# Attention, soft mixture of experts and squared-ReLU layer on one core: nine multiplications by the softmax reciprocals move from VectorE to GpSimd

## The chip, the cores and the metric

The kernel runs on one core of a Trainium2 chip. The metric is the device time of one execution in microseconds (us). TensorE (PE in the profile; PEld is its weight load), VectorE (DVE), ScalarE (ACT), GpSimd (POOL) and SyncE (SP) each work through a queue of their own in program order and wait for each other on semaphores. GpSimd's queue here also issues DMAs.

## The reference

Three layers follow one another, all in float32.

```python
scores = scale * np.matmul(q, k.transpose(0, 1, 3, 2))       # batch 4, heads 12, seq 448, head_dim 64
scores = cap * np.tanh(scores / cap)
attn = np.exp(scores - np.max(scores, axis=-1, keepdims=True))
attn = attn / (np.sum(attn, axis=-1, keepdims=True) + 1e-09)
out = np.matmul(attn, v)                                     # then x: (4*448, 768)

logits = x @ phi                                             # 768 -> 32 slots, 8 experts of 4
d = softmax(logits, axis=0); c = softmax(logits, axis=1)
slot_out[e] = np.maximum((d.T @ x)[e] @ w1[e], 0) @ w2[e]    # 768 -> 1024 -> 768
y = c @ slot_out

h = np.maximum(y @ w_in, 0); out = (h * h) @ w_out           # 768 -> 2048 -> 768
```

## The kernel before

**Attention** is a loop over 24 pairs of heads, 6 pairs (`HP`) to a batch, written by hand as a software pipeline: the order in the source is the order in each engine's queue. In iteration i it works on five pairs at once:

- pair i: the scores (L318, L323), tanh and exp on ScalarE (L325, L327, L333), and the first half of the column sums on VectorE (`sums`, L339);
- pair i+1: VectorE splits q and k into a high part (`prep_hi`, L294) and a rest (`prep_lo`, L300), and GpSimd copies four 64x64 corners of them into the tail tile (L306);
- pair i-1: the second half of the column sums (`sums`, L343), the products with v (`pv`, L355 and L352), and `den`: matmuls with a block of ones give the denominators (L365), VectorE takes the reciprocals (L372), and four DMAs on SP spread them over the partitions into the tile `bc` (L378);
- pair i-2: `take`, in which ScalarE copies the products out of PSUM into `xt` (L403);
- pair i-3: `norm` multiplies `xt` by `bc` in place, 128x448 (L410). Inside `den(i-1)`, right behind its matmuls, TensorE multiplies the normed `xt` by phi (`logits_mm`, L427); both write the same PSUM tile `dn`. Later in the iteration `to_tokens` transposes `xt` (L419).

On VectorE `norm(i-3)` stands ahead of the second sums of pair i-1 (L343), then come L294 and L300 for pair i+1, the reciprocals of pair i-1, and the addition of the logits of pair i-3 (L437, L439). On TensorE the denominators that need those sums stand right ahead of the logits that need `norm`. GpSimd's queue holds, in each iteration, the four casts of pair i+1 (L306) and then the eight DMAs that load v of pair i+1 (six at L285, two at L289, `load_v`); the DMAs of iteration i-1 stand ahead of the casts of iteration i.

When the last pair of a batch has its logits (i % 6 == 2, from i = 8 on), the steps of the batch's end are strewn over that iteration and the three after it (`batch_end`): maxima of the logits and an exp, a transpose and its copy (L478) in i = 9, 15, 21, and two gathers on TensorE (L490) with an accumulation on VectorE (L501, L503) in i = 10, 11, 16, 17, 22, 23. In most iterations VectorE also decodes a part of a packed weight tile (L192, L201, L204, L209).

**The experts** follow: their weights are streamed by DMAs on SP into a ring of buffers (L166), and TensorE uses them as they land (L860, L885). **The last layer** (L969 to L1089) is TensorE's.

The call that the change touches stands in the loop right behind `take`:

```python
                if old:
                    take(i - 2)
                if tok:
                    norm(i - 3)
                if prv:
                    sums(i - 1, 1)
```

Of the kernel before, what the change touches and what calls it, by code (L numbers as in the profile page):

```python
# [14 lines left out]
ALU = mybir.AluOpType  # L15
# [27 lines left out]
def softcap_attention_soft_moe_relu2(  # L43
# [11 lines left out]
    nc = tc.nc  # L55
    B, HP, D, _, _, S = qk.shape
# [173 lines left out]
    with ExitStack() as att:  # L230
# [34 lines left out]
        def load(i):  # L265
            b, two, h = heads_of(i)
            t = raw_tile(i)
            nc.sync.dma_start(out=t, in_=qk[b, two, :, :, h].rearrange("j d r s -> (j d) r s"))
            st["raw", i] = t
# [4 lines left out]
        def load_v(i):  # L274
            b, two, hh = heads_of(i)
            src = v[b, two, :, hh].rearrange("j q c d -> q j c d")
            va = vp.tile([P, NG, 2, D], F32, tag="va", name=f"va{i}")
            vt = vtail[i % 2]
            for g in range(NG):
                at, end = g * P, (g + 1) * P  # L280
                while at < end:
                    c, q = divmod(at, CP)
                    n = min(CP - q, end - at)
                    r = at - g * P
                    nc.gpsimd.dma_start(out=va[r:r + n, g], in_=src[q:q + n, :, c])  # L285
                    at += n
            for h in range(2):
                rows = slice(D * h, D * h + D)
                nc.gpsimd.dma_start(out=vt[rows, rows], in_=src[CP - D:, h, C - 1])  # L289
            st["v", i] = va, vt  # L290

        def prep_hi(i):
            hi = qkp.tile([P, 2, S], F32R, tag="hi", name=f"hi{i}")
            nc.vector.tensor_copy(hi, st["raw", i])  # L294
            st["hi", i] = hi

        def prep_lo(i):
            hi = st["hi", i]
            lo = qkp.tile([P, 2, S], F32R, tag="lo", name=f"lo{i}")
            nc.vector.tensor_tensor(out=lo, in0=st.pop(("raw", i)), in1=hi.bitcast(F32), op=ALU.subtract)  # L300
            st["lo", i] = lo
            kt = ktail[i % 2]
            for n, t in enumerate((hi, lo)):
                for h in range(2):
                    rows = slice(D * h, D * h + D)
                    nc.gpsimd.tensor_copy(kt[rows, n, rows], t[rows, 1, PT:].bitcast(F32))  # L306

        def scores(i, g):
            hi, lo = st["hi", i], st["lo", i]
            sc = ps_s.tile([P, 2, 512], F32, tag="sc", name=f"sc{i}_{g}")  # L310
            terms = ((0, hi), (1, hi), (0, lo))
            if g % 2 == 0:
                st["p", i, g // 2] = p_tile(i, g // 2)
            p = st["p", i, g // 2][:, g % 2]
            for n, (w, x) in enumerate(terms):
                flags = dict(start=n == 0, stop=n == len(terms) - 1)
                if g == NG:
                    nc.tensor.matmul(sc[:, 0, :S], ktail[i % 2][:, w], x[:, 0], **flags)  # L318
                    continue
                for h in range(2):  # L320
                    rows = slice(D * h, D * h + D)
                    k = (hi, lo)[w][rows, 1, g * P:(g + 1) * P]
                    nc.tensor.matmul(sc[:, h, :S], k, x[rows, 0], **flags)  # L323
            if g == NG:
                nc.scalar.activation(p[:, 0], sc[:, 0, :S], AF.Tanh, scale=tsc)  # L325
            else:
                nc.scalar.activation(p, sc[:, :, :S], AF.Tanh, scale=tsc)  # L327
# [75 lines left out]
            nc.scalar.copy(xt, st.pop(("pv", i))[:, :S])  # L403
            st["xt", i] = xt

        def norm(i):
            bc = st.pop(("bc", i))
            if ("xt", i) in st:
                xt = st["xt", i]
                nc.vector.tensor_tensor(out=xt, in0=xt, in1=bc, op=ALU.mult)  # L410
                return
            nc.vector.tensor_tensor(out=bc, in0=st.pop(("pv", i))[:, :S], in1=bc, op=ALU.mult)
            st["xt", i] = bc
# [168 lines left out]
        with tc.If(flag_v == 0, preferred_fallthrough_block=False) as cond:  # L582
            load_v(0)
            prep_hi(0)
            prep_lo(0)
            load(2)
            for i in range(NPAIR):
                last = i == NPAIR - 1
                prv, old, tok = (i >= n for n in (1, 2, 3))
                scores(i, 0)  # L590
                scores(i, 1)
                exps(i, 0)
                if old:
                    take(i - 2)
                if tok:
                    norm(i - 3)
                if prv:
                    sums(i - 1, 1)
                if old:
                    den_rows(i - 2)  # L600
                if not last:
                    prep_hi(i + 1)
                    prep_lo(i + 1)
                if i + 3 < NPAIR:
                    load(i + 3)
                if prv:
                    for g in range(NG):
                        pv(i - 1, g)
                    den(i - 1, i - 3 if tok else None)
                if tok:  # L610
                    logits_add(i - 3)
                    if (i - 3) % HP == HP - 1:
                        late = batch_end((i - 3) // HP)
                        late.pop(0)()
                    elif (i - 3) % HP in (1, 2):
                        step()
                if i in range(4, 16, 2):
                    load_weight(NPAIR // 2 - 1 + (i - 4) // 4, part=i // 2 % 2)
                if i == NPAIR - 2:
                    load_weight(NB - 2, part=0)  # L620
                    load_weight(NB - 2, part=1)
                if (i, 2) in dsteps:
                    dsteps.pop((i, 2))()
                if i < 2 * len(early) and i % 2 == 0:
                    x = early[i // 2]
                    load_raw(*x, ring[NB - 1 - i // 2 % 2][:, :WSZ])
                    dsteps[i + 1, 1] = lambda x=x: decode_a(x)
                    dsteps[i + 2, 0] = lambda x=x: decode_b(x, nc.vector)
                    dsteps[i + 2, 1] = lambda x=x: decode_c([x], (0, 1))
                    dsteps[i + 3, 0] = lambda x=x: decode_c([x], (2,))  # L630
                    dsteps[i + 4, 2] = lambda x=x: store(x)
                if i % 2 and i < NPAIR - 1:
                    load_weight(i // 2)
                if (i, 0) in dsteps:
                    dsteps.pop((i, 0))()
                scores(i, 2)
                scores(i, 3)
                exps(i, 1)
                if prv:
                    pv(i - 1, NG)  # L640
                sums(i, 0)
                if tok:
                    to_tokens(i - 3)
                    if (i - 3) % HP == 0:
                        step()
                if not last:
                    load_v(i + 1)
                if i == 2:
                    load_weight(NB + 1)
                if i == NPAIR - 2:  # L650
                    load_weight(NB)
                    load_weight(NB - 3, part=0)
                    load_weight(NB - 3, part=1)
                if tok and (i - 3) % HP == HP - 1:
                    late.pop(0)()
                    steps.extend(late)
                if (i, 1) in dsteps:
                    dsteps.pop((i, 1))()
                if i == NPAIR - 4:
                    load_weight(NB - 1)  # L660
            assert not dsteps
            assert not steps
            n = NPAIR - 1
            pv(n, 0)
            pv(n, 1)
            sums(n, 1)
            den_rows(n - 1)
            load_weight(NB + 2, nc.scalar)
            pv(n, 2)
            pv(n, 3)  # L670
            norm(n - 2)
            norm(n - 1)
            den(n)
            to_tokens(n - 2, nc.scalar)
            logits(n - 2)
            den_rows(n)
            logits(n - 1, False)
            load_weight(NB + 3, nc.scalar)
            load_weight(NB + 4, nc.scalar)
            norm(n)  # L680
            to_tokens(n - 1, nc.scalar)
            logits(n, False)
            last_end(True)

        with cond.Else():
# [8 lines left out]
            for i in range(NPAIR):  # L694
# [9 lines left out]
                for h in range(2):  # L704
                    for c in range(C):
# [10 lines left out]
                            out=e, in0=e, scalar1=mx, scalar2=None, op0=ALU.subtract  # L716
# [23 lines left out]
                xt = bcp.tile([P, S], F32, tag="bc", name=f"gxt{i}")  # L740
# [438 lines left out]
```

## Time and profile before

| | |
|---|---|
| median of 3 runs | 555.55 us (555.1 to 557.49) |
| the profiled execution | 557.33 us, of which the span from the first to the last instruction is 555.5 us |
| busy: TensorE, VectorE, ScalarE, GpSimd | 94%, 60%, 60%, 29% of the span |
| granted TensorE clock, mean | 0.997 |
| attention, by the profile's times | from the start to about 209 us |

Times in the rows are microseconds from the span's start. Busy shares are means over stages that have different limits, so what an engine is worth in one stage is read from that stage. Iteration i of the attention loop is taken from one first score matmul to the next: i = 9 begins at 78.41 us, i = 10 at 86.15, i = 15 at 125.14, i = 16 at 133.34, i = 21 at 172.34.

### The profile page before, as it was taken

The page shows a single profiled execution, that of the slowest core. Times are in us where ns is not written, and L with a number is a line of the kernel's source. Part 1 is how long each engine was busy: PE and PEld are TensorE (multiplying, and loading weights), DVE is VectorE, ACT ScalarE, POOL GpSimd, SP SyncE. Part 2 cuts the span into 40 slices and gives each one's busy share as a digit, 9 for nine tenths or more (in the row PEclk, how much of TensorE's full clock was granted, in tenths as well). Part 3 has the DMA queues.
Part 4 walks back from the last instruction along what each step waited for, and adds up shares of the span by engine and source line. Part 5 has one row for each costly group of instructions (what it writes and reads, how often), then busy time and mean ns, then how long its engine had stood idle before and what let it go on. Part 6 is the DMA issues. An engine that isn't in the chain of part 4 may idle for free.

```text
span 555.5 us, 10533 instructions
## 1 busy us (share of the span) xinstructions
PE 520.5 (94%) x4068; PEld 357.7 (64%) x4068; DVE 331.4 (60%) x529; ACT 332.3 (60%) x467; POOL 160.3 (29%) x347
## 2 busy tenths in 40 slices
PE   2999999999999989888679999999999999999997
PEld 1555556655655645444236888888888888788885
DVE  2499999999999765440018989889641231322111
ACT  2899999999899840000026677766654455633342
POOL 6987889788878601000000000000000000000000
PEclk9999999999999998999999999999999999999999
DMA  3688987899878799999998544551030110001002
GB/s 108 186 268 265 258 252 228 253 272 273 239 251 234 205 361 416 418 413 416 416 401 336 170 145 163 196 181 57 1 114 0 40 75 1 0 20 38 1 1 113
DMA packets 46249, 108.16 MB, mean 195 GB/s; under 512 B 19440, under 2 KB 28272, under 8 KB 46192
## 3 DMA queue, kind: packets, MB, share of 16 engines
q1 hardware_dynamic: 39472, 99.14, 50.9%
q0 software_dynamic: 6144, 5.52, 4.6%
q10 hardware_dynamic: 576, 2.75, 1.2%
q8 instruction: 34, 0.56, 0.4%
q14 instruction: 23, 0.19, 0.1%
HBM read 94.47 MB, written 7.86 MB: 184 GB/s over the span
## 4 chain that ended last, share of the span: by engine, by line
PE 78%; DMA 12%; ACT 3%; DVE 3%; issue 3%; SPq 0%; ACTq 0%; DVEq 0%
PE y L1089 35%; PE pv L355 9%; PE sc L323 8%; DMA rb<-in_w_dram 8%; PE y L1026 4%; DMA r<-in_w_dram 3%; PE dn L365 3%; PE sc L318 3%; PE pv L352 3%; PE h L969 2%; PE y L1030 2%; PE xm L419 1%; PE so L885 1%; ACT r L327 1%; PE u L490 1%
## 5 line engine op out<-in xcount | busy, mean ns | idle before, releaser
L1089 PE MATMUL y<-gh,wo 128*128 128x512 f32 x576 | 179.0, 393 | 0.4 <-ACT part L1036 0.4
L1089 PEld LDWEIGHTS y<-gh,wo 128*128 128x128 f32 x576 | 106.5, 188 | 24.2 <-issue 1.4
L1089 PE MATMUL y<-gl,wo 128*128 128x512 f32 x288 | 111.6, 390 | 0.0
L982 DVE TENSOR_TENSOR gl<-r,gh 128x512 fp32r<-128x512 f32 (+1 forms) x64 | 40.0, 625 | 112.7 <-ACT gh L981 110.8
L285 POOL DMA_DIRECT2D va<-in_v_dram x144 | 86.7, 609 | 2.5 <-issue 2.4
L973 ACT ACTIVATE r<-h 128x512 f32<-128x512 f32 (+1 forms) x64 | 34.8, 544 | 80.1 <-PE h L969 80.1
L327 ACT ACTIVATE r<-sc,tsc 128x896 f32<-128x896 f32 x72 | 69.5, 998 | 17.5 <-PE sc L323 17.4
L333 ACT ACTIVATE r<-r,cabs 128x1792 f32<-128x1792 f32 (+1 forms) x48 | 77.1, 1606 | 1.6
L1089 PEld LDWEIGHTS y<-gl,wo 128*128 128x128 f32 x288 | 54.1, 188 | 11.6
L355 PE MATMUL pv<-r,va 128*64 128x448 f32 x288 | 60.3, 553 | 0.0
L323 PE MATMUL sc<-hi 64*128 64x448 f32 x144 | 32.7, 449 | 10.9 <-DVE hi L294 10.1
L867 ACT ACTIVATE hs<-ph 128x256 f32<-128x256 f32 x8 | 3.1, 383 | 65.8 <-PE ph L860 65.8
L355 PEld LDWEIGHTS pv<-r,va 128*64 128x64 f32 x288 | 18.6, 138 | 29.9 <-issue 22.5
L980 ACT ACTIVATE r<-r 128x512 f32<-128x512 f32 (+1 forms) x62 | 35.8, 577 | 2.0
L981 ACT CAST gh<-r 128x512 fp32r<-128x512 f32 (+1 forms) x62 | 35.1, 566 | 2.0
L306 POOL CAST ktail<-hi 64x64 fp32r<-64x64 f32 x48 | 27.0, 562 | 22.6 <-DVE hi L294 20.8
L339 DVE SCALAR_TENSOR_TENSOR psum<-r,gcol 128x896 f32<-128x896 f32 x24 | 27.3, 1139 | 3.5 <-POOL ktail L306 3.5
L885 PE MATMUL so<-rb,ht 128*32 128x256 f32 x298 | 24.9, 382 | 4.2 <-DVE ht L873 2.1
L289 POOL DMA_DIRECT2D vtail<-in_v_dram x48 | 28.0, 587 | 2.2 <-issue 2.2
L300 DVE TENSOR_TENSOR lo<-r,hi 128x896 fp32r<-128x896 f32 x24 | 26.9, 1120 | 2.8 <-POOL ktail L306 0.5
L343 DVE TENSOR_TENSOR psum<-psum,r 128x896 f32<-128x896 f32 x24 | 26.0, 1085 | 4.1 <-ACT r L333 3.9
L873 DVE COPY ht<-px 128x32 f32<-128x32 f32 x8 | 1.5, 192 | 44.7 <-PE px L870 36.2
(195 smaller groups left out, 819.6 us busy)
## 6 DMA issues: line engine op xcount, KB each, us to landing
rb<-in_w_dram SPq DMA_DIRECT2D x41, 768.0 KB, 14.3
r<-in_qk_dram SPq DMA_DIRECT2D x24, 448.0 KB, 4.7
r<-in_w_out_dram SPq DMA_DIRECT2D x13, 768.0 KB, 4.3
r<-in_w_in_dram SPq DMA_DIRECT2D x9, 768.0 KB, 4.3
r<-in_w_dram SPq DMA_DIRECT2D x7, 896.0 KB, 17.2
rb<-in_w_in_dram SPq DMA_DIRECT2D x7, 768.0 KB, 6.8
bc<-rc SPq DMA_DIRECT2D x88, 56.0 KB, 4.1
rb<-in_w_dram SPq DMA_DIRECT2D x12, 384.0 KB, 5.2
```

Of the source, the lines that this page charges most:

```text
L285: nc.gpsimd.dma_start(out=va[r:r + n, g], in_=src[q:q + n, :, c])
L289: nc.gpsimd.dma_start(out=vt[rows, rows], in_=src[CP - D:, h, C - 1])
L323: nc.tensor.matmul(sc[:, h, :S], k, x[rows, 0], **flags)
L327: nc.scalar.activation(p, sc[:, :, :S], AF.Tanh, scale=tsc)
L333: nc.scalar.activation(p, p, AF.Exp, scale=cabs)
L355: nc.tensor.matmul(o[D * h:D * h + D, :S], va[:, g, h], p[:, h], start=(g == 0), stop=False,)
L885: nc.tensor.matmul(so[32 * j:32 * j + 32, :UNIT], ht[:, ft, :], weights(EU * e + EU // 2 + u), start=(e == 0 and ft == 0), stop=(e == NE - ...
L973: nc.scalar.activation(r[:, :n], h[:, :n], AF.Relu)
L980: nc.scalar.activation(r[:, :n], r[:, :n], AF.Square)
L981: nc.scalar.copy(gh[:, :n], r[:, :n])
L982: eng.tensor_tensor(out=gl[:, :n], in0=r[:, :n], in1=gh[:, :n].bitcast(F32), op=ALU.subtract)
L1089: nc.tensor.matmul(y[:, :nn], whl[ft][:, wi, ds], gx[:, :nn], start=(ft == first and t == 0), stop=(ft == end - 1 and t == 2),)
```

## The change

`norm` takes an engine, and the loop passes GpSimd when i > 6 and i % 6 >= 3: that is i = 9, 10, 11, 15, 16, 17, 21, 22 and 23, and so pairs 6, 7, 8, 12, 13, 14, 18, 19 and 20. The other fifteen multiplications stay on VectorE.

```diff
-        def norm(i):
+        def norm(i, eng=nc.vector):
             bc = st.pop(("bc", i))
             if ("xt", i) in st:
                 xt = st["xt", i]
-                nc.vector.tensor_tensor(out=xt, in0=xt, in1=bc, op=ALU.mult)
+                eng.tensor_tensor(out=xt, in0=xt, in1=bc, op=ALU.mult)
                 return
...
                 if tok:
-                    norm(i - 3)
+                    norm(i - 3, nc.gpsimd if i > HP and i % HP >= HP // 2 else nc.vector)
```

On VectorE in iteration 15 (pair 12; `xt_1603` is its product, `psum_187` the sums of pair 14, `hi_1716` and `lo_1718` pair 16) the order was

```order
L201 TENSOR_SCALAR rb_99<-rb_99 128x768
L204 SCALAR_TENSOR_TENSOR rb_99<-rb_84,rb_99 128x768
L410 TENSOR_TENSOR xt_1603<-xt_1603,bc_1545 128x448
L343 TENSOR_TENSOR psum_187<-psum_187,r_79 128x896
L294 CAST hi_1716<-r_75 128x896
L300 TENSOR_TENSOR lo_1718<-r_75,hi_1716 128x896
L372 RECIPROCAL rc_1749<-dn_1732 128x112
```

and now L410 is gone from it, the rest standing as before. On GpSimd, in the same iteration, the order now is

```order
203 L410 TENSOR_TENSOR xt_1603<-xt_1603,bc_1545 128x448
204 L306 CAST ktail_189<-hi_1716 64x64 x2
205 L306 CAST ktail_189<-lo_1718 64x64 x2
206 L285 DMA va_1786<-in_v_dram 112x2x64
207 L285 DMA va_1786<-in_v_dram 16x2x64
208 L285 DMA va_1786<-in_v_dram 96x2x64
209 L285 DMA va_1786<-in_v_dram 32x2x64
210 L285 DMA va_1786<-in_v_dram 80x2x64
211 L285 DMA va_1786<-in_v_dram 48x2x64
212 L289 DMA vtail_191<-in_v_dram 64x64 x2
213 L410 TENSOR_TENSOR xt_1712<-xt_1712,bc_1642 128x448
```

where the multiplication (row 203) stands behind the eight DMAs that load v of pair 15 and ahead of the casts of pair 16, and the next one (row 213) behind the eight DMAs of pair 16. On TensorE, with the semaphores that rows wait for, the piece of difference at the same place is

```order
 L365 MATMUL dn_1732<-psum_187,onesp 32x112 [waits DVE_49]
 L365 MATMUL dn_1732<-psum_187,onesp 32x112 x7
-L427 MATMUL dn_1732<-xt_1603,phi_sb 32x112 x4
+L427 MATMUL dn_1732<-xt_1603,phi_sb 32x112 [waits Pool_49]
+L427 MATMUL dn_1732<-xt_1603,phi_sb 32x112 x3
 L323 MATMUL sc_2_1759<-hi_1607 128x448 [waits Activation_49]
```

so the logits, which had been covered by the wait of the denominators for VectorE, now have a wait of their own for GpSimd, and the scores of the iteration's second half stand behind them. The same happens in the other eight iterations; no other row of any queue moves.

## Rows read from the trace of the kernel before

**Rows 1.** The page: the chain that ended last, its shares of the span.

```profile
PE 78%; DMA 12%; ACT 3%; DVE 3%; issue 3%; SPq 0%; ACTq 0%; DVEq 0%
```

**Rows 2.** The chain in order of time, 20 to 270 us: start, length, what.

```profile
128.04 0.62 DVE xt L410
128.66 1.01 DVE psum L343
129.72 0.59 PE dn L365 x16
...
175.09 0.62 DVE xt L410
```

**Rows 3.** GpSimd's timeline, undisturbed casts and iteration 9: start, length, instruction, count [idle before].

```profile
22.55 0.53 POOL L306 CAST ktail<-hi 64x64 fp32r<-64x64 f32 x2
...
80.11 1.06 POOL L289 DMA_DIRECT2D vtail<-in_v_dram  x2
83.08 1.27 POOL L306 CAST ktail<-hi 64x64 fp32r<-64x64 f32 x2 [1.91 <-DVE hi L294]
```

**Rows 4.** VectorE's timeline, iteration 9.

```profile
80.86 0.62 DVE L410 TENSOR_TENSOR xt<-xt,bc 128x448 f32<-128x448 f32 x1
81.39 1.09 DVE L343 TENSOR_TENSOR psum<-psum,r 128x896 f32<-128x896 f32 x1
82.39 0.62 DVE L294 CAST hi<-r 128x896 fp32r<-128x896 f32 x1
83.12 1.14 DVE L300 TENSOR_TENSOR lo<-r,hi 128x896 fp32r<-128x896 f32 x1
```

**Rows 5.** TensorE's timeline, iteration 9.

```profile
82.53 0.59 PE L365 MATMUL dn<-psum,onesp 128*32 128x112 f32 x16
82.94 0.38 PE L427 MATMUL dn<-xt,phi_sb 128*32 128x112 f32 x8
```

**Rows 6.** Groups by form, GpSimd: names, shapes, count, busy us, mean ns, idle before.

```profile
L553 POOL TENSOR_SCALAR u_sb<-u_sb,alpha,fb 128x256 f32<-128x256 f32 x1 | 0.8, 783 | 18.6 <-DVE fb L550 18.6
...
L122 POOL TENSOR_TENSOR seld<-seld,ident 128x32 f32<-128x32 f32 x2 | 0.5, 250 | 0.2
L122 POOL TENSOR_TENSOR selh<-selh,ident 128x2 f32<-128x2 f32 x2 | 0.4, 195 | 0.2
```

**Rows 7.** GpSimd's timeline, iterations 10 and 11: the last two v loads before each.

```profile
88.38 1.07 POOL L289 DMA_DIRECT2D vtail<-in_v_dram  x2
...
95.92 1.06 POOL L289 DMA_DIRECT2D vtail<-in_v_dram  x2
```

**Rows 8.** VectorE's timeline, iteration 10.

```profile
88.33 1.08 DVE L343 TENSOR_TENSOR psum<-psum,r 128x896 f32<-128x896 f32 x1
89.33 0.62 DVE L294 CAST hi<-r 128x896 fp32r<-128x896 f32 x1
90.05 1.14 DVE L300 TENSOR_TENSOR lo<-r,hi 128x896 fp32r<-128x896 f32 x1
```

**Rows 9.** TensorE's timeline, iterations 10 and 11: the logits.

```profile
90.57 0.37 PE L427 MATMUL dn<-xt,phi_sb 128*32 128x112 f32 x8
...
98.97 0.37 PE L427 MATMUL dn<-xt,phi_sb 128*32 128x112 f32 x8
```

**Rows 10.** GpSimd's timeline, iteration 15.

```profile
126.73 0.54 POOL L289 DMA_DIRECT2D vtail<-in_v_dram  x1
129.50 0.80 POOL L289 DMA_DIRECT2D vtail<-in_v_dram  x1 [2.23 <-issue]
130.35 1.44 POOL L306 CAST ktail<-hi 64x64 fp32r<-64x64 f32 x2
```

**Rows 11.** VectorE's and TensorE's timelines, iteration 15.

```profile
130.30 1.09 DVE L300 TENSOR_TENSOR lo<-r,hi 128x896 fp32r<-128x896 f32 x1
...
130.12 0.38 PE L427 MATMUL dn<-xt,phi_sb 128*32 128x112 f32 x8
```

**Rows 12.** Busy time of each engine, DMA share and GB/s, in one stretch of the experts.

```profile
230.00:260.00 30.00, 26.47 (x376) 14.40 (x371) 8.88 (x26) 2.15 (x6) 0.93 (x3) 1.00 1.02 416
```

## Prediction

> **What bounds the kernel now.** I read the chain that ended last first. Over the whole span 78% of it is TensorE [rows 1]; in attention it goes from matmul to matmul, and the few pieces that are not TensorE's are what a change there can win. Two of them are VectorE's: in iterations 15 and 21 the chain passes through `norm` (0.62 us) and the second sums behind it, and only then to the denominators, which begin at 129.72 in iteration 15 [rows 2]. The chain puts a DMA ahead of `norm` there, but VectorE has no idle time before it: it is late because of its own backlog. In iteration 9 the sums end at 81.39 + 1.09 = 82.48 and the denominators start at 82.53 [rows 4, 5], a wait of some 0.1. Everywhere else in the nine iterations TensorE runs without one. So taking `norm` off VectorE can bring at most its 81.39 - 80.86 = 0.53 [rows 4] in iterations 15 and 21 and 0.1 in iteration 9: 1.1 us.
>
> Next I read the queue that gets the work. GpSimd reaches the new instruction only when its eight DMAs are out, and that is late in the iteration: at 80.11 + 1.06 = 81.17 in iteration 9 [rows 3], where the logits that need the product start at 82.94 [rows 5]; at 89.45 in iteration 10 [rows 7], logits at 90.57 [rows 9]; at 130.30 in iteration 15 [rows 10], logits at 130.12 [rows 11]. VectorE starts its own at 80.86 and 128.04 [rows 2, 4]. The product's inputs are there in both cases, so these times decide.
>
> **How long it takes on GpSimd.** Before has no such instruction of this size. GpSimd's own additions with two inputs take 195 ns at 2 columns and 250 ns at 32 [rows 6]: 1.83 ns a column, so 448 columns are estimated at 195 + 446 x 1.83 = 1010 ns. Below, the bound is VectorE's 0.62; above, the 783 ns of 256 columns [rows 6], part of it probably waiting, give 1.37. I take 1.0, the estimate from the same kind of instruction.
>
> **Who may run beside it.** Two casts take 0.53 us alone and 1.27 when VectorE runs the subtraction for `lo` [rows 3]: that began at 83.12 and ended at 84.26 [rows 4], and the casts ended at 84.35. GpSimd stands still until VectorE's instruction with two inputs from SBUF is over. Now `norm` on GpSimd becomes ready where VectorE runs three long SBUF instructions in a row: L343, L294 and L300. That is the heart of the forecast.
>
> What no row shows is who goes first when L343 ends while GpSimd waits and L294 already stands behind it; so I price both. The Trainium skill ("SBUF — State Buffer", section "A bandwidth-pool intuition that's wrong") says that the blocked side waits until the VectorE instruction's end plus about 115 ns. By that GpSimd would go first each time and the sum below would be its low end; the rows on the casts agree with the 0.1 us, but behind those came an instruction of another kind.
>
> **The sum.** All by delays of the logits on TensorE, behind which the rest of the iteration stands.
>
> - Iteration 9: VectorE now starts L343 at 80.86, to 81.95; GpSimd, ready at 81.17, waits. If it goes next, it ends at 82.95 and the logits start about 83.05: 0.1 late. If L294 goes next (to 82.48), GpSimd ends at 83.5 and the logits are 0.65 late.
> - Iteration 10: after the product, GpSimd's casts run into L300, so its next DMAs are out some 0.65 later than before, at 90.1. L300 stands there at about 90.05 - 0.53 + 0.5 = 90.0, to 91.1 [rows 8] (it was itself held by the product in iteration 9). If GpSimd just gets in first, the product ends at 91.1; if not, at 92.1. Against 90.57 that is 0.6 to 1.65 late, with what iteration 9 lost in it.
> - Iteration 11: GpSimd is some 1.3 late, at 96.98 + 1.3 = 98.3 [rows 7], the product at 99.3; the logits are due at 98.97 [rows 9] plus the delay of about 1.1. In time; 0 to 0.45 if a VectorE instruction goes first.
> - Iteration 15: the second of the last two v loads starts 2.23 us after the first ended, with nothing in the profile that it waits for [rows 10]. It is the 128th DMA of this queue (8 for each of pairs 0 to 15), and I take it that it stalls again. GpSimd is then ready at 130.1 to 130.3, inside L300, which now runs from 129.77 to 130.86 (0.53 earlier than [rows 11]). The product ends at 131.9 and the logits start at 131.96 instead of 130.12: 1.85 late. The 0.53 won on the denominators is lost in this wait. Without the stall it would be about 0.6.
> - Iterations 16 and 17: GpSimd is 0.8 late and TensorE 1.85, so mostly in time: 0 to 0.6 and 0 to 0.45.
> - Iterations 21 and 22 repeat 9 and 10: 0.6 to 1.65. Iteration 23 has no L294 and L300 any more: 0.
>
> Together 0.6 to 2.1, 1.85 to 2.9 and 0.6 to 1.65: 3.05 to 6.65, middle 4.85. With the product at 0.62 or 1.37 the ends move by about 0.4 for each of the five places that count, to 1.1 and 8.5.
>
> At nothing I cost: the four DMAs that spread the reciprocals (SP), which follow the later reciprocals by the same delay and still land an iteration ahead of use; the lost wait of the scores for the casts, which the logits' wait covers; and the v loads, up to 1.3 late, which have most of an iteration until `pv`. If that cover is gone, a v load late by 1 us costs 1 us once.
>
> The delay is handed on whole: the experts' weights stream at 416 GB/s with the DMA engines full [rows 12], but the loads that begin it wait for tiles that attention frees, so the stream starts later by the same time.
>
> The profiled execution took 557.33 us, so its like would take 562.1; against the median of the runs, 555.55, I forecast **560.3 us**.
>
> **The rivals.**
>
> 1. *The product is in time and VectorE's relief counts.* If the 128th DMA does not stall and GpSimd gets its turn at each end of a VectorE instruction, L343's 0.53 comes through in iterations 15 and 21 and 0.1 in iteration 9: 555.55 - 1.1 = 554.4. It decides at a start 1.05 us ahead of the logits: 81.17 is early enough for 82.94 less the 0.1. For it: GpSimd is idle for 1.91 us there [rows 3]. Against it: that idle time is just when VectorE has L343 and L294. Not slower.
> 2. *No contention, only the stall.* If an instruction of GpSimd as long as this one shares with VectorE, only iteration 15 is late, by 131.3 - 130.12 = 1.2, with the rest about even: 555.55 + 1.0 = 556.5. Against it stand the casts [rows 3].
> 3. *VectorE is held instead.* When GpSimd starts first, VectorE waits for the whole product. `lo` took 1.14 beside a cast that had begun first and 1.09 otherwise [rows 4, 11], so VectorE does wait, by little, since a cast is short. With the product, VectorE loses up to 1.0 where it saved 0.53, nine times 0.47 = 4.2; where VectorE has a backlog that comes on top: 555.55 + 4.8 + 4.2 = 564.5. The Trainium skill ("SBUF — State Buffer", section "Who interferes with whom") has this rule: whoever issues first gets the shared ports for the whole instruction. No row here shows it for a long GpSimd instruction.
>
> **How the numbers follow.** Forecast 0.66, rival 1 0.09, rival 2 0.16, rival 3 0.09. The range 556.0 to 563.0 takes in rival 2 and the forecast with its bounds but for their last tails, and leaves out rival 1 and most of rival 3. A measurement of this kernel can tell 0.5%, 2.8 us, from no change. Slower by more: the forecast without its low tail, and rival 3, 0.70. Within: both other rivals and that tail, 0.28. Faster by more: 0.02, since all that VectorE can give back is 1.1 us.
>
> **What would show it.** In the profile after, L410 on GpSimd should take 1.0 us where VectorE is quiet and up to 2 where it started inside L343 or L300; TensorE should show idle time before L427, released by GpSimd, of some 1.8 us in iteration 15 and 0.5 to 1 in 10 and 22; L343 in iteration 15 should end half a microsecond earlier relative to the iteration; the 2.2 us stall should stand again before the 128th DMA. The forecast is wrong if no wait for GpSimd stands before L427 (rival 1), if it stands in iteration 15 alone (rival 2), or if TensorE waits for VectorE's L343 or L300 instead (rival 3).

## The result, and the profile after

The changed kernel takes **560.69 us** against 556.84 for the kernel before in the same comparison: a ratio of 1.0082, with a 95% interval of 1.0064 to 1.0099, so 3.6 to 5.5 us slower. The forecast was 560.3. The execution that was profiled first was a disturbed one (569.63 us; of the kernel before, 5 of 97 executions took 564.49 us and more), so the rows below come from the second profile of the same kernel (the first experiment, 560.86 us, span 559.0).

The page, busy time, and the chain's shares of the span, to set beside [rows 1]:

```profile
PE 520.8 (93%) x4068; PEld 357.8 (64%) x4068; DVE 331.6 (59%) x520; ACT 332.6 (59%) x467; POOL 172.9 (31%) x356
...
PE 71%; DMA 13%; DVE 5%; POOL 3%; issue 3%; ACT 3%; SPq 0%; POOLq 0%; ACTq 0%; DVEq 0%
```

GpSimd, which was nowhere among the shares of before, now has 3% of the chain, and VectorE has more than it had, not less. The waits view, attention from 75 to 200 us (us in total, times, longest), says where:

```profile
PE dn L427 <- POOL xt L410: 5.0, 4, 2.1
```

TensorE stands in front of the logits for GpSimd's product, four times, 5.0 us in all. TensorE's timeline has the four places (iterations 10, 15, 21 and 22), and in iteration 15 the denominators ahead of the logits:

```profile
91.40 0.40 PE L427 MATMUL dn<-xt,phi_sb 128*32 128x112 f32 x8 [1.22 <-POOL xt L410]
...
130.29 0.59 PE L365 MATMUL dn<-psum,onesp 128*32 128x112 f32 x16
133.01 0.40 PE L427 MATMUL dn<-xt,phi_sb 128*32 128x112 f32 x8 [2.13 <-POOL xt L410]
...
180.12 0.40 PE L427 MATMUL dn<-xt,phi_sb 128*32 128x112 f32 x8 [0.31 <-POOL xt L410]
...
189.31 0.40 PE L427 MATMUL dn<-xt,phi_sb 128*32 128x112 f32 x8 [1.35 <-POOL xt L410]
```

Iteration 15 begins at 126.23 here, so the denominators stand 4.06 us into it where they stood 129.72 - 125.14 = 4.58 before [rows 2]: the 0.52 of relief did arrive. The logits behind them then stand at 6.78 where [rows 11] have 4.98.

GpSimd's timeline, iterations 9, 10, 11, 15 and 22, beside [rows 3, 7, 10]:

```profile
79.44 1.06 POOL L289 DMA_DIRECT2D vtail<-in_v_dram  x2
80.57 1.71 POOL L410 TENSOR_TENSOR xt<-xt,bc 128x448 f32<-128x448 f32 x1
82.83 1.28 POOL L306 CAST ktail<-hi 64x64 fp32r<-64x64 f32 x2 [0.55 <-DVE hi L294]
...
88.17 1.10 POOL L289 DMA_DIRECT2D vtail<-in_v_dram  x2
89.33 2.02 POOL L410 TENSOR_TENSOR xt<-xt,bc 128x448 f32<-128x448 f32 x1
...
97.38 1.30 POOL L410 TENSOR_TENSOR xt<-xt,bc 128x448 f32<-128x448 f32 x1
...
130.36 0.53 POOL L289 DMA_DIRECT2D vtail<-in_v_dram  x1 [1.97 <-DMA bc<-rc]
130.96 2.00 POOL L410 TENSOR_TENSOR xt<-xt,bc 128x448 f32<-128x448 f32 x1
...
185.95 1.23 POOL L289 DMA_DIRECT2D vtail<-in_v_dram  x2
187.25 2.01 POOL L410 TENSOR_TENSOR xt<-xt,bc 128x448 f32<-128x448 f32 x1
```

and VectorE's at the same places, beside [rows 4, 8, 11]:

```profile
80.19 1.08 DVE L343 TENSOR_TENSOR psum<-psum,r 128x896 f32<-128x896 f32 x1
81.19 1.57 DVE L294 CAST hi<-r 128x896 fp32r<-128x896 f32 x1
82.86 1.14 DVE L300 TENSOR_TENSOR lo<-r,hi 128x896 fp32r<-128x896 f32 x1
...
88.54 0.62 DVE L294 CAST hi<-r 128x896 fp32r<-128x896 f32 x1
89.27 1.09 DVE L300 TENSOR_TENSOR lo<-r,hi 128x896 fp32r<-128x896 f32 x1
...
97.59 2.04 DVE L343 TENSOR_TENSOR psum<-psum,r 128x896 f32<-128x896 f32 x1
...
130.16 0.62 DVE L294 CAST hi<-r 128x896 fp32r<-128x896 f32 x1
130.88 1.09 DVE L300 TENSOR_TENSOR lo<-r,hi 128x896 fp32r<-128x896 f32 x1
...
186.46 0.61 DVE L294 CAST hi<-r 128x896 fp32r<-128x896 f32 x1
187.18 1.09 DVE L300 TENSOR_TENSOR lo<-r,hi 128x896 fp32r<-128x896 f32 x1
```

Three things are to be seen. In iteration 9 the product began inside L343 (to 81.27), ended 1.0 behind it at 82.28, and held the cast L294 for 1.57 us where it took 0.62. In iterations 10, 15 and 22 it began 0.06 to 0.08 us behind the start of L300, and ended 1.0 behind L300's end: 2.0 us for one product. In iteration 11 it was VectorE that waited: the product had begun first, and the second sums L343 took 2.04 instead of 1.08, which put the denominators 0.23 later into the iteration. The gap of 1.97 ahead of the last v load in iteration 15 stands where [rows 10] had 2.23; the name behind the arrow is an inference and differs between runs.

The lengths of the iterations, from one first score matmul to the next, give the account in us:

| iteration | before | after | growth | forecast |
|---|---|---|---|---|
| 9 | 7.74 | 7.83 | 0.09 | 0.1 to 0.65 |
| 10 | 8.40 | 9.85 | 1.45 | with 9: 0.6 to 1.65 |
| 11 | 7.98 | 8.22 | 0.24 | 0 to 0.45 |
| 15 | 8.20 | 10.02 | 1.82 | 1.85 |
| 16, 17 | 8.42, 7.98 | 8.40, 7.98 | 0 | 0 to 1.05 |
| 21, 22 | 8.06, 8.42 | 8.15, 9.95 | 1.62 | 0.6 to 1.65 |

Together 5.2 us in this execution, where the comparison measured 3.6 to 5.5. The four waits for GpSimd are 5.0 of it; the 0.24 of iteration 11 is VectorE's wait.

### The profile page after: what moved, and what is told of

The parts are those of the page before. It is cut to its first block, busy times and chain, and to the rows that moved or that the text cites. A ratio compares the mean times of both kernels' runs of the same rounds, so it can differ in the third digit from the quotient of the medians.

```text
span 567.8 us, 10551 instructions
## 1 busy us (share of the span) xinstructions
PE 522.7 (92%) x4068; PEld 358.6 (63%) x4068; DVE 332.1 (58%) x520; ACT 332.9 (59%) x467; POOL 185.6 (33%) x356
## 4 chain that ended last, share of the span: by engine, by line
PE 70%; DMA 11%; POOL 9%; DVE 4%; issue 3%; ACT 2%; SPq 1%; ACTq 0%; POOLq 0%; DVEq 0%
PE y L1089 34%; DMA rb<-in_w_dram 7%; PE pv L355 6%; PE sc L323 5%; PE y L1026 4%; POOL va L285 4%; PE so L885 3%; POOL ktail L306 3%; DMA r<-in_w_out_dram 3%; PE ph L860 2%; PE h L969 2%; PE pv L352 2%; PE dn L365 2%; PE sc L318 2%; PE y L1030 2%
## 5 line engine op out<-in xcount | busy, mean ns | idle before, releaser
L285 POOL DMA_DIRECT2D va<-in_v_dram x144 | 86.6, 608 | 2.6 <-issue 2.6
L306 POOL CAST ktail<-hi 64x64 fp32r<-64x64 f32 x48 | 30.8, 642 | 12.3 <-DVE hi L294 10.4
L343 DVE TENSOR_TENSOR psum<-psum,r 128x896 f32<-128x896 f32 x24 | 28.0, 1167 | 4.2 <-ACT r L333 4.1
L372 DVE RECIPROCAL rc<-dn 128x112 f32<-128x112 f32 x24 | 20.5, 854 | 16.4 <-PE dn L427 13.2
L885 PE MATMUL so<-rb,ht 128*32 128x256 f32 x298 | 26.5, 400 | 3.3 <-DVE ht L873 2.1
L339 DVE SCALAR_TENSOR_TENSOR psum<-r,gcol 128x896 f32<-128x896 f32 x24 | 27.4, 1143 | 3.7 <-ACT r L333 3.6
L300 DVE TENSOR_TENSOR lo<-r,hi 128x896 fp32r<-128x896 f32 x24 | 27.3, 1139 | 2.9 <-POOL ktail L306 0.5
```

Of the source, the lines that this page charges most:

```text
L885: nc.tensor.matmul(so[32 * j:32 * j + 32, :UNIT], ht[:, ft, :], weights(EU * e + EU // 2 + u), start=(e == 0 and ft == 0), stop=(e == NE - ...
```

## The experiments

The forecast's theory (A below): GpSimd comes to the product late, behind its DMAs, shares the way to SBUF with VectorE there, and TensorE's logits wait. The rivals: it is the stall before the 128th DMA alone (C); VectorE is what is held (B); or GpSimd's lost time shows elsewhere, as late loads of v (D). In the table, "growth" is the sum of what iterations 9 to 11, 15 to 17, 21 and 22 gained over before in the profiled execution. What lies in other iterations is said with the run.

| run | us | ratio to before, 95% | growth | waits of the logits for GpSimd |
|---|---|---|---|---|
| e1_after_again | 561.93 | 1.0103 (1.0061 to 1.0144) | 5.2 | 1.22, 2.13, 0.31, 1.35 |
| e2_first_of_three | 559.09 | 1.0048 (1.0026 to 1.0070) | 1.3 | 1.52, 0.30 |
| e3_ahead_of_v | 563.30 | 1.0106 (1.0059 to 1.0152) | 4.5 | one, 1.7 |
| e4_v0_from_sp | 562.58, one execution | | 8.0 | 1.23, 2.21, 0.30, 1.35 |
| e5_unused_product | 561.53 | 1.0083 (1.0038 to 1.0128) | 0.4 | none |
| e6_ahead_of_vtail | 557.62 | 1.0032 (1.0015 to 1.0048) | 1.9 | none |
| e7_sums_first | 554.45 | 0.9975 (0.9955 to 0.9995) | -0.8 | none |
| e8_half | 561.12 | 1.0090 (1.0071 to 1.0110) | 4.1 | 0.88, 1.48, 1.01 |
| e9_two_memsets | 556.03 | 1.0001 (0.9984 to 1.0018) | -0.2 | none |
| e10_sums_first_all | 555.40 | 0.9993 (0.9979 to 1.0006) | -0.9 | none |
| e11_vtail_from_sp | 557.78 | 1.0034 (1.0015 to 1.0053) | 0.8 | none |
| e12_sums_first_again | 555.37 | 0.9985 (0.9971 to 0.9998) | -1.0 | none |

### The changed kernel once more

No edit: a second profile, and a second comparison.

> The changed kernel as it is, for a profile and a time beside the other runs of this call. Theory A (the product reaches GpSimd's turn late, behind the v loads and held by VectorE's L343, L294 and L300, and TensorE's logits wait for it): TensorE idle before L427, released by GpSimd, of 1.8 us in iteration 15, 0.1 to 0.65 in 9 and 21, 0.5 to 1 in 10 and 22; 3 to 6.6 us slower than before in all. Theory B (VectorE is the one held, for as long as GpSimd reads): the idle time stands before TensorE's denominators or scores instead, released by VectorE. Theory C (only the stalled 128th DMA counts): a wait in iteration 15 alone, 1 to 1.5 us in all.

Measured: the rows above. L410 on GpSimd takes 1.30 to 2.02 us, median 1.76, as the tile's view has it:

```profile
L410 POOL TENSOR_TENSOR xt<-xt,bc x9: 1302/1762/2017, 80.6 to 194.9; 128x448 f32<-128x448 f32 x9
```

### Only the first iteration of the three

```diff
-norm(i - 3, nc.gpsimd if i > HP and i % HP >= HP // 2 else nc.vector)
+norm(i - 3, nc.gpsimd if i > HP and i % HP == HP // 2 else nc.vector)
```

> GpSimd multiplies in iterations 9, 15 and 21 alone, VectorE in the other six. Theory A: 0.1 to 0.65 each in 9 and 21 and 1.85 in 15, so 2.0 to 3.2 us slower than before, and the rest of the whole change's loss lies in the second and third of the three. Theory B: a third of the whole, about 1.5. Theory C: as much as the whole change, 1 to 1.5 by its own price.

Measured: +2.7 us (1.4 to 3.9). The waits in 10 and 22 are gone with the products there; 15 still waits 1.52 and 21 waits 0.30. So iterations 10 and 22 have costs of their own, and the stall does not make up the whole loss. The profiled execution (557.86) lay below the median of its kind, and its growth of 1.3 leaves out 0.54 in iteration 14, at whose end TensorE waited for ScalarE.

### The stall moved

```diff
-            load_v(0)
+            load_v(0, nc.sync)
```

with `load_v(i, eng=nc.gpsimd)` issuing all eight DMAs by `eng`.

> The changed kernel, with the eight DMAs that load v of pair 0 issued by SP instead of GpSimd, so that the 128th DMA of GpSimd's queue is the last of pair 16 instead of pair 15. If the 2 us stall belongs to the 128th DMA, it moves from before pair 15's last to before pair 16's last, the logits wait under 0.7 us in iteration 15, and the wait of 1 to 1.5 us moves to iteration 16. If it belongs to the place in the program or to the time, it stays before pair 15's last.

GpSimd's timeline, iteration 16, and TensorE's there:

```profile
138.86 0.53 POOL L289 DMA_DIRECT2D vtail<-in_v_dram  x1 [2.22 <-DMA bc<-rc]
139.46 1.12 POOL L410 TENSOR_TENSOR xt<-xt,bc 128x448 f32<-128x448 f32 x1
```

```profile
140.63 0.40 PE L427 MATMUL dn<-xt,phi_sb 128*32 128x112 f32 x8 [2.21 <-POOL xt L410]
```

With pair 0's eight loads taken off the queue, its 128th DMA is pair 16's last, and the gap of 2.2 us stands there: it goes by what the queue issued before, not by the place in the program. (The run "The last two loads from SP" below shows that the number 128 itself is not what counts.) The wait of 2.1 moved with it, out of iteration 15 into 16. The gap thus makes one wait long; those in 10, 21 and 22 are as they were. Iteration 16 grew by 3.97, more than its wait, and the rest of the 8.0 was not followed up. In 15 the product now comes ahead of L343 and holds it for 2.03, so the denominators wait 0.79 for the second sums.

### Ahead of the eight loads

```diff
-if tok:
+if tok and not (i > HP and i % HP >= HP // 2):
     norm(i - 3)
...
+if i + 1 > HP and (i + 1) % HP >= HP // 2:
+    norm(i - 2, nc.gpsimd)
 load_v(i + 1)
```

> The same nine multiplications on GpSimd, but put ahead of the eight v loads of the iteration before instead of behind them, some 5 us earlier in its queue. Theory A: no wait of the logits for GpSimd is left, and VectorE's relief of 0.53 us in iterations 15 and 21 comes through: 0 to 1.1 us faster than before. Theory B: the product then runs beside VectorE's L339 and holds it or is held, so it stays 2 to 4 us slower than before. Theory C: no loss, as theory A.

Measured: +5.9 us (3.3 to 8.4), no gain over the change, where the theories had at most 4. The product is in time in all places but one, and other waits take the place of the logits'. GpSimd's timeline, then VectorE's and TensorE's, iteration 15:

```profile
125.28 1.13 POOL L410 TENSOR_TENSOR xt<-xt,bc 128x448 f32<-128x448 f32 x1 [0.91 <-ACT xt L403]
...
125.41 1.42 DVE L192 TENSOR_SCALAR rb<-rb 128x768 f32<-128x768 f32 x1
...
131.01 0.59 PE L365 MATMUL dn<-psum,onesp 128*32 128x112 f32 x16 [0.60 <-DVE psum L343]
```

Here GpSimd went first: its product took 1.13, and VectorE's L192, 0.55 elsewhere, took 1.42. The 0.87 lost is more than the 0.53 that the change took from VectorE, and the denominators wait 0.60 for the sums. That is the smaller part: iteration 15 grew by 0.23 only, iteration 21 by 3.6. GpSimd's casts in iteration 20, which take some 0.5 undisturbed, and the logits in 21:

```profile
167.20 3.90 POOL L306 CAST ktail<-hi 64x64 fp32r<-64x64 f32 x2
```

```profile
181.31 0.40 PE L427 MATMUL dn<-xt,phi_sb 128*32 128x112 f32 x8 [1.67 <-POOL xt L410]
```

GpSimd has fallen behind there, and besides, the v loads now stand behind the product. The waits view:

```profile
PE pv L355 <- DMA va<-in_v_dram: 3.3, 3, 2.4
```

TensorE waits for v three times, 3.3 us in all: 0.31 and 0.62 in iterations 20 and 21, and 2.40 in 23, which the sum in the table leaves out. How much of the late casts and loads the new order brings about was not separated.

### Ahead of the last two loads only

The call stands inside `load_v`, behind the six loads at L285:

```diff
+            if i > HP and i % HP >= HP // 2:
+                norm(i - 3, nc.gpsimd)
```

> The nine products on GpSimd, ahead of the last two of the eight v loads instead of behind them, 1.1 us earlier in its queue and ahead of the stalled 128th DMA. If the loss comes from GpSimd beginning 0.06 us behind VectorE's L300 in iterations 10, 15 and 22, the products now go in after L343 at the latest: no wait of the logits in 10 and 22, 0 to 0.6 us in 15, and in all 0 to 1.5 us slower than before. If GpSimd's lateness as such is what costs (each VectorE instruction ahead of it is served first), the waits stay and so does a loss of 3 us or more.

GpSimd's, VectorE's and TensorE's timelines, iteration 15 (lines from here on are two higher, so L412 is the product and L345 the second sums):

```profile
126.12 1.82 POOL L412 TENSOR_TENSOR xt<-xt,bc 128x448 f32<-128x448 f32 x1
...
125.97 0.96 DVE L204 SCALAR_TENSOR_TENSOR rb<-rb,rb 128x768 uint32<-128x768 uint32 x1
126.85 2.03 DVE L345 TENSOR_TENSOR psum<-psum,r 128x896 f32<-128x896 f32 x1
...
128.94 0.59 PE L367 MATMUL dn<-psum,onesp 128*32 128x112 f32 x16 [0.69 <-DVE psum L345]
```

No logits wait any more, and 2.8 of the 4.6 us that the change lost come back, but the kernel is still 0.8 to 2.7 us slower than before, more in the middle than the 1.5 that the first theory had at most. The product began inside L204, and when that ended at 126.93 it had the next turn: L345 took 2.03 instead of 1.08. VectorE lost 0.95 to save 0.53, and the denominators wait longer (0.69) than before the change (0.36). Two more things stand in this profile. In iteration 10 the product began inside L345 (86.46 to 87.54) and still let the cast L296 go first:

```profile
87.11 1.97 POOL L412 TENSOR_TENSOR xt<-xt,bc 128x448 f32<-128x448 f32 x1
...
87.46 0.61 DVE L296 CAST hi<-r 128x896 fp32r<-128x896 f32 x1
88.18 1.85 DVE L302 TENSOR_TENSOR lo<-r,hi 128x896 fp32r<-128x896 f32 x1
```

It ended 1.0 behind L296's end and held L302 (1.85 instead of 1.09); so it went in iterations 16 and 22. And the last two v loads now stand behind the product. In iteration 23 TensorE waits for them, 1.5 us that the growth of 1.9 leaves out:

```profile
PE pv L354 <- DMA vtail<-in_v_dram: 1.5, 1, 1.5
```

### The last two loads from SP

```diff
-nc.gpsimd.dma_start(out=vt[rows, rows], in_=src[CP - D:, h, C - 1])
+nc.sync.dma_start(out=vt[rows, rows], in_=src[CP - D:, h, C - 1])
```

> The changed kernel, with the two small v loads of each pair (L289) issued by SP instead of GpSimd: GpSimd reaches each product some 1.1 us earlier, has that much more time in each iteration, and its 128th DMA falls into another iteration. Theory A and D: no waits of the logits in 10, 15 and 22, no casts of over 2.5 us, and between 1 us faster and 1 us slower than before, with VectorE still held a little in 9, 15 and 21. Theory B: 2 to 4 us slower than before, with TensorE's waits for VectorE.

Measured: +1.9 us, no wait of the logits, iteration 15 shorter by 0.58, iterations 9 and 21 longer by 0.4 (11 and 17 by 0.2 and 0.3), where the denominators wait for VectorE:

```profile
PE dn L365 <- DVE psum L343: 0.9, 2, 0.6
```

Iteration 14 lasts 8.46, with TensorE waiting 0.85 for ScalarE, which the sum in the table leaves out; ScalarE had waited for a weight tile to land, and iteration 14 is longer in e2 and e7 too (0.54 and 0.21), so this may be chance. The time lies between what the two theories had. As in the run before, the loss shrinks when the product is in time, and VectorE's hold is what remains at 9 and 21.

GpSimd's queue issues six DMAs for each pair here. Its 128th starts without a gap, and a gap stands before its 114th, the last of pair 18:

```profile
152.45 0.57 POOL L285 DMA_DIRECT2D va<-in_v_dram  x1 [1.68 <-issue]
```

### Half of the columns

```diff
+if eng is nc.gpsimd:
+    nc.vector.tensor_tensor(out=xt[:, :S // 2], in0=xt[:, :S // 2], in1=bc[:, :S // 2], op=ALU.mult)
+    eng.tensor_tensor(out=xt[:, S // 2:], in0=xt[:, S // 2:], in1=bc[:, S // 2:], op=ALU.mult)
+    return
```

> The changed kernel, with the columns halved: VectorE multiplies the first 224 columns where it did before, GpSimd the other 224. If the price is the length of the product behind L300, each of the waits in 10, 15 and 22 shrinks by some 0.45 us, and the kernel is 2.5 to 4 us slower than before. If it is the place in the queue and what stands ahead, the waits stay within 0.2 us of the whole product's 1.2, 2.1 and 1.35, and the loss at 4 us or more.

Measured: +5.0 us (3.9 to 6.1, four executions), no less than the change itself, as for the place in the queue. But the waits became shorter by 0.34, 0.65 and 0.34, and that in 21 is gone, as for the length: 3.4 us of waits are left of 5.0, and the growth is 4.1 instead of 5.2. VectorE gave up half of its relief. So about a third of the waits goes with the product's size; the rest stays, since the half product too begins behind L300 in 10, 15 and 22 and ends only 0.5 behind L300's end.

### A product that nobody needs

VectorE multiplies as before; GpSimd then squares the tile of reciprocals, which is not used again.

```diff
+bc_ = st["bc", i - 3]
+norm(i - 3)
+if i > HP and i % HP >= HP // 2:
+    nc.gpsimd.tensor_tensor(out=bc_, in0=bc_, in1=bc_, op=ALU.mult)
```

> VectorE multiplies in all iterations, as before, and GpSimd in the nine iterations runs a product of the same size at the same place of its queue that nothing waits for: it squares the reciprocals' tile, which nobody reads any more. Theory A (what costs is that TensorE's logits wait for GpSimd): most of the 4.6 us goes, 0 to 1.5 us slower than before, with no idle time before L427. Theory B (VectorE and the v loads are held back by the product, whoever uses it): 3 to 5 us slower than before, with TensorE's waits for VectorE.

Measured: three executions took 557.57 to 558.21 (1.2 to 1.8 more than before), three took 564.84 to 571.49, and the profile is of the one of 564.84. Nothing waits for this product, yet the three short ones are slower than before too. By what way, no profile shows; VectorE's instructions are held beside the product in the long one (L339 takes 1.82 in iteration 17 instead of 1.14). That the product brings the three longer times about is not shown. What the profile has of the 564.84 is late loads of v. GpSimd's timeline, iteration 18, then VectorE's, then TensorE's in iteration 19:

```profile
149.38 1.19 POOL L599 TENSOR_TENSOR bc<-bc 128x448 f32<-128x448 f32 x1
150.52 3.77 POOL L306 CAST ktail<-hi 64x64 fp32r<-64x64 f32 x2
...
152.04 0.61 DVE L410 TENSOR_TENSOR xt<-xt,bc 128x448 f32<-128x448 f32 x1
152.57 1.08 DVE L343 TENSOR_TENSOR psum<-psum,r 128x896 f32<-128x896 f32 x1
153.57 0.61 DVE L294 CAST hi<-r 128x896 fp32r<-128x896 f32 x1
...
161.25 1.78 PE L355 MATMUL pv<-r,va 128*64 128x448 f32 x8 [2.16 <-DMA va<-in_v_dram]
164.12 0.97 PE L355 MATMUL pv<-r,va 128*64 128x448 f32 x4 [1.10 <-DMA va<-in_v_dram]
```

Two casts that take 0.53 undisturbed [rows 3] take 3.77, the second of them 2.62, until VectorE's run of three is over. The eight loads of v behind them come late, and TensorE waits 3.3 us for v: iteration 19 lasts 11.12 us, where a regular one has 7.53. In iteration 23 it waits 2.7 us more for v. What makes GpSimd late enough for this in some executions and not in others was not found.

### GpSimd's time without its reading

The same place, but GpSimd fills the tile twice instead of multiplying: it writes and reads nothing.

```diff
+for _ in range(2):
+    nc.gpsimd.memset(bc_, 0.0)
```

> VectorE multiplies everywhere, as before, and GpSimd in the nine iterations writes zeros twice over the reciprocals' tile, which nobody reads any more: about 1.0 us of GpSimd that reads nothing. Theory D (GpSimd has no time left: what it does more makes its casts meet VectorE's run of L410, L343 and L294 and its v loads late, as with the unused product): casts of over 2.5 us, waits of the products with v for their load, and 1 to 5 us slower than before, spread as with the unused product. Theory B (the contention of reads with VectorE): 0 to 1 us slower, no such casts.

GpSimd's and VectorE's timelines, iteration 9:

```profile
80.97 1.00 POOL L600 MEMSET bc<- 128x448 f32 x2 [0.41 <-issue]
...
81.77 0.67 DVE L294 CAST hi<-r 128x896 fp32r<-128x896 f32 x1
```

One microsecond more of GpSimd in nine iterations, at the same place, costs nothing that the time shows: 1.0001 (0.9984 to 1.0018). L343 and L300 beside a fill take their usual 1.08 and 1.09, and a fill that begins inside L343 takes its usual 0.47. With the cast L294 the fills do take turns: L294 takes 0.67 here and up to 0.81 in iteration 17 (1.57 beside the product), and a fill behind it 0.88 and 1.01 in iterations 10 and 22. So GpSimd's time as such is free. What is left to cost is the product's reading beside VectorE's instructions with two inputs, its length beside L294, and the wait for its result.

### VectorE alone, in another order

Against the kernel before, the second sums stand ahead of the product, both on VectorE, in iterations 9, 15 and 21:

```diff
+if i > HP and i % HP == HP // 2:
+    sums(i - 1, 1)
+    norm(i - 3)
+else:
     if tok:
         norm(i - 3)
     if prv:
         sums(i - 1, 1)
```

> All products on VectorE, as before, but in iterations 9, 15 and 21 behind the second sums (L343) instead of ahead of them, so that VectorE's relief is had without GpSimd. If the waits of the denominators for L343 are what there is to win: iteration 15 shorter by 0.3 to 0.5 us and iteration 21 by 0.2 to 0.4, and 0.5 to 1.0 us faster than before in all, too little to be told from no change by the time alone. If something else keeps these iterations long, their length stays at 8.2 and 8.06 us.

VectorE's and TensorE's timelines, iteration 15:

```profile
127.16 1.09 DVE L343 TENSOR_TENSOR psum<-psum,r 128x896 f32<-128x896 f32 x1
128.16 0.62 DVE L410 TENSOR_TENSOR xt<-xt,bc 128x448 f32<-128x448 f32 x1
...
128.51 0.57 PE L365 MATMUL dn<-psum,onesp 128*32 128x112 f32 x16
```

The denominators no longer wait, and the logits behind them, at 128.89, find the product done at 128.78. Iterations 15 and 21 are shorter by 0.58 and 0.37, and the kernel takes 0.9975 of before. Again, with more executions:

> The second sums ahead of VectorE's product in iterations 9, 15 and 21, timed a second time, since all iterations done so came out within the interval of no change. By the lengths of iterations 9, 15 and 21 in the profiles it should be 0.9 to 1.0 us faster than before (ratio 0.998); a ratio of 1.000 or more would say that the shorter iterations are given back later, one of 0.9975 that there is more in it than these three.

Measured: 0.9985 (0.9971 to 0.9998), iterations 15 and 21 shorter by 0.47 and 0.38. In every iteration instead of three:

> As before, with the second sums ahead of the product on VectorE in all iterations instead of in 9, 15 and 21. Elsewhere VectorE is not late, so nothing more should come: the same as with the three alone, 0.5 to 2 us faster than before. If the product then comes too late for the logits in other iterations, TensorE's waits for L410 before L427 show it and the gain is gone.

Measured: 0.9993 (0.9979 to 1.0006), which can't be told from before or from the run with three. Both comparisons of the version with three put it ahead of before, by 0.8 and 1.4 us, with intervals that end just short of none (0.1 and 0.3), and so ahead of the changed kernel by more than 4: it has the relief that [rows 2] promised without GpSimd.

## Why the prediction was right

**Bound and relief: right.** The 0.53 of VectorE did come through to the denominators in iteration 15 (0.52), and was lost in the logits' wait right behind them, as forecast. The order of VectorE alone shows that the sum of such relief is about a microsecond: 0.8 and 1.4 measured, 1.1 forecast.

**When GpSimd gets there: right.** It reached the product behind its DMAs, and the gap before the 128th DMA stood again (1.97); e4 moved it. That it belongs to the 128th as such was a guess that held for these eight DMAs a pair and not for the six of e11, where it stood before the 114th. Iteration 15 grew by 1.82 against 1.85.

**The product's duration: the size a little off.** I took 1.0 from small additions. Where GpSimd goes first it takes 1.12 (e4) and 1.13 (e3); behind a VectorE instruction it ends 1.0 after that one's end.

**Who goes first: open in the forecast, and not settled by one rule.** In iterations 9, 17 and 21 the product began inside L343 and went ahead of L294, which was held: 9 and 21 stand at their low ends. This agrees with the rule of the Trainium skill ("SBUF — State Buffer", section "A bandwidth-pool intuition that's wrong") that the blocked side goes on when the other instruction ends; 1.0 us behind L343's end the product was over. In e6 the same wait ended otherwise: in 10, 16 and 22 L296 went ahead of the waiting product. What decides between the two is not shown.

The low end of the whole sum, which I drew from that rule, did not come, for another reason: in 10, 15 and 22 the product stands 0.06 to 0.08 us behind the start of L300, each time, and pays for the whole of it. I had left 10 and 22 as ties, between 0.6 and 1.65 together with 9 and 21; they came out at the upper end, 1.54 and 1.62. The rows bear on why it is each time the same. The last v load ends 0.11 us behind L294's end in all three (89.16 and 89.27, 130.78 and 130.89, 187.07 and 187.18), and that is when L300 begins. In the kernel before, six last v loads begin 0.07 to 0.29 ahead of L294; each ends 0.10 to 0.11 behind L294's end and takes 0.80 to 1.01 instead of 0.54. So L294 can hold such a load, and lets it go too late for the product to come ahead of L300. In 10 and 22 the load was lengthened, to 0.57 and 0.70; in 15 it took its usual 0.53, and there the meeting may be chance. No run tried this by itself.

**Iteration 11: in the range by luck.** I had 0 to 0.45 for logits that come late. They were in time; the 0.24 is the denominators' wait for L343, which the product held. This is rival 3's mechanism.

**At nothing: right for this kernel, not by much.** No wait for v is seen in the profile of e1, and the spread of the reciprocals never mattered. But the cover that I gave the v loads, most of an iteration, was gone in e3, e5 and, at iteration 23, in e6.

**Handed on whole: right, as far as one execution shows.** The sum over attention is 5.2 in one execution, the comparison 3.9 as a difference of medians and 4.6 as a ratio; the two are not told apart. The profiled execution is only 3.5 longer than that of before, which had 0.7 more ahead of iteration 9 and 1.0 more behind the start of 23. Against that of e9, whose time is as before, those two stretches agree within 0.1, and the 5.3 that lie between the starts of 9 and 23 are all there at the end (559.0 and 553.8).

**The number: closer than the mechanism earns.** The forecast added 4.8 to a median of 555.55; measured are 3.9 on one of 556.84. That 560.69 lies 0.4 from 560.3 is in part luck. (The sum as it stands, 555.55 + 4.85, gives 560.4.)

**The rivals.** Rival 1 fell: the logits wait in four places. Rival 2 fell: three of them have no stall, and meeting L300 makes 2.0 of 1.12. Rival 3's mechanism is real, but smaller than its price: VectorE was held by up to 0.95 in e6, and there, without the logits' wait, it made most of a loss of 1.8 us out of the hoped-for gain. In the changed kernel five of the nine products held L343, L294 or L300, by 0.75 to 0.95; it reached TensorE in iteration 11 alone.

## What to carry to other kernels

Before a step goes to an idle engine, look at when that engine's queue reaches it and what the other engine runs at that moment: here an instruction of 0.6 us became one of 2.0, because it stood behind DMA issues and then beside VectorE's longest reads. Idle time in GpSimd's queue was free here only for work that reads nothing and that nobody waits for (the two fills), so put the moved step's due time beside its earliest start, in each iteration. And when one engine's backlog delays another, first try the order on that engine: two instructions swapped gave what the move was to give.

## What the hardware showed that was not expected

- A product on GpSimd and VectorE's long instructions take turns, whole instructions at a time, in both directions: GpSimd 2.0 instead of 1.12, L294 1.57 instead of 0.62, L343 2.04 instead of 1.08, L192 1.42 instead of 0.55. The Trainium skill says so ("SBUF — State Buffer", section "Who interferes with whom": whoever issues first has the shared ports for the whole instruction), and these numbers agree.
- The end of a VectorE instruction is not always the waiting side's turn. The product got it ahead of L294 in 9, 17 and 21 of the changed kernel, and not in 10, 16 and 22 of e6. A cast of e5 began at 151.67, 0.37 ahead of L410, and was held through L410, L343 and L294, for 2.62 us. What decides stays open.
- L294 also held the issue of a DMA on GpSimd's queue, in six places of the kernel before, where that began 0.07 to 0.29 us ahead of it: 0.80 to 1.01 us for one that takes 0.54, with its end 0.10 to 0.11 behind the end of L294. Two that began 0.41 and 0.42 ahead took their usual 0.54.
- Filling a tile on GpSimd beside L343 and L300 cost neither engine anything; beside the cast L294 a fill took up to 1.01 instead of 0.47.
- GpSimd's queue has one gap of 1.4 to 2.2 us ahead of a DMA in attention: ahead of the 128th in the kernel before (2.23), the changed one (1.97) and e4 (2.22, one pair later), ahead of the 114th in e11 (1.68), where each pair has six. In e6, where the product stands ahead of the 127th and 128th, there is none. What is counted is not shown.
